# Attention rows stored in a power-of-two scale, and a running sum in the expert selection

## The chip, the cores and the metric

The kernel runs on one core of one Trainium2 chip. The metric is device time in microseconds of that core, median of several runs. One execution was also taken with the hardware profiler; its trace is what all rows below come from.

## The reference

Clustered attention is followed by a mixture of experts with a capacity. Batch 4, 8 heads, 768 tokens, head size 64, 16 clusters; 3072 tokens of 512 numbers go to 8 experts of width 1024, at most 80 tokens each.

```python
mask = q_assign[:, :, :, None] == k_assign[:, :, None, :]
scores = np.where(mask, scale * np.matmul(q, k.transpose(0, 1, 3, 2)), -1e9)
attn = np.exp(scores - np.max(scores, axis=-1, keepdims=True))
attn = attn / (np.sum(attn, axis=-1, keepdims=True) + 1e-09)
x = np.matmul(attn, v)                      # then (B*S, H*D)
...
logits = x @ w_gate                         # expert_idx = argmax, gate_w = its softmax
for e in range(E):
    tok_idx = np.where(expert_idx == e)[0]
    if len(tok_idx) > capacity:             # keep the capacity largest gate_w
        gw = gate_w[tok_idx]
        tok_idx = tok_idx[np.argpartition(-gw, capacity)[:capacity]]
    h = np.maximum(x[tok_idx] @ w1[e], 0.0)
    out[tok_idx] = gate_w[tok_idx, None] * (h @ w2[e])
```

## The kernel before

Products that need more than fp16 gives are made from two halves: a high part rounded to fp16, and the rest. `scale` (L253) makes for each batch a power of two `s` for v, from the sum of its squares, so that the halves stay within fp16; `split_v` multiplies v with it.

**Attention.** For each of 32 heads and 6 blocks of 128 keys, TensorE makes scores, ACT two exponentials (`exps`, L575: fp32 and fp16), and their difference `ll` is made on POOL or, for the tiles that `inplace` (L569) names, on DVE (`rests`, L589). TensorE sums with both halves (`av`, L596). `normalise` (L614) divides by the sum of weights (times `s`, which undoes v's scale) and stores the rows of x to a buffer `xs` in HBM. `gates` (L643) makes the gate value `G` and the one-hot `OH` of each token's expert.

**Selection.** To keep the 80 largest gates of each expert, `select` (L732) finds a threshold per expert by digits of the bits of `G`, in five levels (shift 20, 15, 10, 5, 0). `digits` (L671) makes for each level the tables `ge` and `pre` on DVE. In a level TensorE counts over 24 token blocks (L754), DVE turns counts into a digit `nf` (L781), TensorE spreads the digit into `nb` (L784), and DVE marks the tokens still `alive` (L791), which the next level's counts read. `banks` (L740) prepares the next level's `nb`: one product for the base (L744) and one for each digit so far (L746). At the end DVE converts `nb` (L798), makes masks, slot positions and, with TensorE, a table `tb` of what stands in each of the 80 slots: token number, three parts of the gate, a flag (`terms`, L705, makes the factors on POOL). `gi` (L853) are the rows to gather.

**Experts.** One unit per expert (80 rows). `gather` (L1043) is an indirect DMA from POOL. For seven of the eight experts (all but number 1, `native1`) `norms` squares the gathered rows on ACT (L1054), `factors` makes a power of two from that in four small DVE instructions (`power`, L876) and two more (L1063, L1065), `tokens` multiplies and splits into fp16 halves on DVE (L1071, L1072); `turn` transposes on TensorE (L1089), `turned` copies, `hidden` multiplies with w1 (L1118), `relu`, `rest` (`hl`, L1134), `output` with w2 (L1146), `gated` (L1171) applies gate and scales, `scatter` writes by indirect DMA (L1176). Weights come in chunks of 512 KB (`load_w`, L902): w1 needs statistics (L918, summed by L923), a scale, and a split. A chunk named in `scaled` is scaled and rounded by two ACT instructions (L1010, L1011) and its low half made by POOL (L1022); any other takes one (L1013 or L1015) and DVE makes the low half (L1024). w2 of the experts 1, 6 and 7 is split as well (L1034 or L1036, and L1040 on POOL or DVE).

**Order.** A planner, `Flow.run` (L1644), runs when the program is built. It gives each step a start by estimated durations and readiness, takes the earliest start on any engine and, among steps of that engine within `wait`, the one with the least offset `at`; so it writes the fixed order of every engine. On the chip each engine works through its order and waits where an operand isn't there. `CFG` holds the offsets (`mix`), how many rooms serve split halves and raw chunks (`slots`), and `bias`, by which the second engine of a step with two (`alt`) must be better. While the selection lane has steps, another lane's DVE step is taken only if it ends before `spare` (L1626), which is when the selection's next step can start plus `mix["spare"]`. Where TensorE would stand longer than `idle`, `fill` (L1600) puts in products that nobody reads (L1506).

Of the kernel before, what the change touches and what calls it, by code (L numbers as in the profile page):

```python
# [7 lines left out]
F32 = mybir.dt.float32  # L8
# [11 lines left out]
CFG = dict(at=dict(rest=0.54, av=3.29, norm=2.04, sm=6.87, exp=0.06, mx=-0.9), stick=0.11, wait=0.128, idle=0.4, dummy=128, bias=1.25,  # L20
           side=(9.43, 16.01, 23.62, 0.88, 28.38), prep=(-1.42, 0.49), lead=(-40, -37.0, -39.26, -37.55, -28.47),
           zero=(-14.97, 0.62, -5.05, 0.1, 4.78, 1.09, -19.25, 0.81, -3.2, 0.25, -13.65, 0.65),
           start=dict(pe=6.1, act=4.8, dve=7.5, pool=2.5, dma=0.0), warm=48, nab=6, lag=3, share=(1, 5), raws=8, slots=(19, 5), native1=(1,),
           native2=(0, 2, 3, 4, 5), early=((5, 0), 185.8), scaled=(3, 4, 5, 6, 7, 11, 13, 14, 17, 19, 20, 21, 22, 24, 27, 29),
           mix=dict(ld=-22.68, st=-20.3, hi1=-1.69, lo1=-10.0, hi2=-14.51, lo2=-5.27, xg=-21.49, xp=-17.51, out=18.38, sc=-11.74, a0=5, a1=4, a2=4, spare=-0.08))
# [11 lines left out]
class Program:  # L37
# [35 lines left out]
    def setup(self):  # L73
# [28 lines left out]
        self.OH = con.tile([P, NT, E], F16, name="OH")  # L102
        self.wgd = con.tile([P, NP, 32], F32, name="wgd")
# [149 lines left out]
    def scale(self, b):  # L253
# [30 lines left out]
        nc.vector.tensor_copy(si[:, 0:1], ti[:, 3:4])  # L284
        nc.vector.scalar_tensor_tensor(ti[:, 4:5], ti[:, 2:3], 127, si[:, 0:1], op0=ALU.add, op1=ALU.subtract)
# [283 lines left out]
    def inplace(self, g):  # L569


        n, d = CFG["share"]
        return (g + 1) * n // d > g * n // d
# [40 lines left out]
    def normalise(self, b, h):  # L614
# [3 lines left out]
        a, (_, _, s, _, ratio) = st["av"], st["s", b]  # L618
# [7 lines left out]
        nc.vector.tensor_scalar(den, a[:, :, X], 1e-9, s, op0=ALU.add, op1=ALU.mult)  # L626
# [5 lines left out]
        nc.vector.scalar_tensor_tensor(l[:, :, :, h], a[:, :, D:X], ratio, rec.unsqueeze(2).broadcast_to([P, NC, E]),  # L632
# [72 lines left out]
    def terms(self):  # L705
# [4 lines left out]
        R = w.tile([P, NT, E, 5], F16, name="R")  # L710
# [15 lines left out]
        put(0, self.tok)  # L726
        nc.gpsimd.tensor_tensor(g[:, :, 2], r1, g[:, :, 1], op=ALU.subtract)
# [4 lines left out]
    def select(self):  # L732
# [7 lines left out]
        def banks(l):  # L740

            q, nb = ps.tile([E, 36], F32, name="q", bufs=2), ps.tile([P, 3 * E + NT], F32, name="nb", bufs=2)
            if l == 0 or self.levels[l][0]:
                nc.tensor.matmul(nb[:, 0:E], lhsT=self.ones[0:E], rhs=self.view["idl"][0:E, 0:E], start=True, stop=False)  # L744
                for i, x in enumerate(nfs):
                    nc.tensor.matmul(nb[:, 0:E], lhsT=x.broadcast_to([E, P]), rhs=ids[i], start=False, stop=False)  # L746
            return q, nb

        for l, (sh, d0, ge, pre) in enumerate(self.levels):
# [6 lines left out]
            if l == 0:  # L756
                yield Step("pe", .025 * known + .2, needs=[("norm", self.B * self.H - 1)])
                q, nb = banks(0)
# [3 lines left out]
            else:  # L762
                yield Step("pe", .025 * NT, also=("dve", .55 if sh else .85), needs=[("ge", l)])
                count(0, NT)
# [8 lines left out]
                if sh == 0:  # L773
                    ti = nb_[:, E:2 * E].bitcast(I32)
                    nc.vector.tensor_scalar(ti, nb_[:, 0:E], 1024.0, None, op0=ALU.mult)
                    top = w.tile([P, E], I32, name="top")
                    nc.vector.tensor_scalar(top, ti, 5, BASE, op0=ALU.logical_shift_left, op1=ALU.bitwise_or)
# [6 lines left out]
            nc.tensor.matmul(nb[:, 0:E], lhsT=nf.broadcast_to([E, P]), rhs=ids[l], start=sh == 0, stop=True)  # L784
            q_, nb_, nj = q, nb, nk
            if sh:
                more = .18 * (l + 2) if self.levels[l + 1][0] else .02
                yield Step("dve", .43, also=("pe", more), needs=[("pre", l)])
# [35 lines left out]
        for m, s0 in enumerate(range(0, cap, P)):  # L824
# [6 lines left out]
            tb = ps.tile([P, E, 5], F32, name="tb", tag="pos")  # L831
# [22 lines left out]
            yield Step("dve", .68, key=("slots", m))  # L854
# [5 lines left out]
            nc.vector.scalar_tensor_tensor(g2, tv[:, :, 1], 1.0 / 1024.0, g1, op0=ALU.mult, op1=ALU.add)  # L860
# [89 lines left out]
    def start(self):  # L950
        self.counts = [0] * 3
        self.hp, self.y, self.xss = {}, {}, {}
        self.width = self.w1.shape[2]
        self.np = self.w1.shape[1] // P, self.w2.shape[1] // P // (self.width // self.w2.shape[2])
        for n in ("raw", "w1s", "ss", "sw", "w2s", "xg", "xt", "xp", "sx", "gs", "h", "yp"):
            setattr(self, n, {})
# [93 lines left out]
    def norms(self, u):  # L1050
        nc, w, Mb, xg = self.nc, self.mw, self.blocks[u[1]][0], self.xg[u]
        xp = self.xp[u] = self.room(4 + self.count(1) % 2, F16).rearrange("p (i d) -> p i d", i=2)
        ss = self.xss[u] = w.tile([P, 1], F32, name="xss", bufs=2)
        nc.scalar.activation(xp[0:Mb, 0], xg[0:Mb], AF.Square, accum_out=ss[0:Mb])  # L1054

    def factors(self, u):

        nc, w, (e, m) = self.nc, self.mw, u
        Mb, gi, si, gate = self.blocks[m]
        ss, bank = self.xss.pop(u), self.misc([P, 8])  # L1060
        self.power(bank[:, 4:6], bank, ss[0:Mb], Mb)
# [101 lines left out]
    def gated(self, u):  # L1163
# [6 lines left out]
        else:  # L1170
            nc.vector.tensor_scalar(y[0:Mb], yp, self.gs[u][0:Mb], self.sw[e][0:Mb, 1:2], op0=ALU.mult, op1=ALU.mult)  # L1171
# [7 lines left out]
    def experts(self):  # L1179
# [401 lines left out]
class Flow:  # L1581
# [62 lines left out]
    def run(self):  # L1644
        while True:
            ready, spare = [], self.spare()
            for n, lane in enumerate(self.lanes):
# [38 lines left out]
            if eng == "pe" and self.idle and start - self.free[eng] > CFG["idle"]:  # L1686
# [113 lines left out]
```

## Time and profile before

| | |
|---|---|
| median of 3 runs | 589.18 us (586.09 to 590.32) |
| the profiled execution | 588.15 us, its span 586.0 us |
| PE (TensorE) busy | 544.2 us, 93% |
| DVE (VectorE) busy | 449.2 us, 77% |
| ACT (ScalarE) busy | 464.8 us, 79% |
| POOL (GpSimd) busy | 423.0 us, 72% |
| mean granted TensorE clock | 0.961 |

Times of the trace count from the start of the span. PE is a matmul, PEld a weight load that can overlap it, SPq a DMA issued from SyncE. A row of a timeline gives start, duration, engine, line, operation, output and inputs with their shapes, how many were merged, and in brackets the idle time of the engine before it with what ended it. Busy time on an engine that is not the bottleneck costs nothing, and a share over the whole span mixes stages with different limits.

### The profile page before, as it was taken

What the parts mean: (1) busy time and instruction counts of PE and PEld (TensorE: products, weight loads), DVE (VectorE), ACT (ScalarE), POOL (GpSimd) and SP (SyncE); (2) the same over time, 40 slices, a digit from 0 to 9 for tenths busy, and PEclk for the clock granted to TensorE, in tenths of its full rate; (3) what the DMA queues carried; (4) which work ended last, traced back from release to release, by engine and by line L of the source; (5) the groups of instructions that cost most, each with busy time, mean ns of one, the idle gap of its engine ahead of it and who ended that gap; (6) DMA issues with size and microseconds to landing.
All of it is one profiled execution on the core that took longest, in us unless ns stands there. A gap on an engine that the chain in (4) does not pass through costs nothing. (4 is left out here: it accounts for less than half of the span.)

```text
span 586.0 us, 16832 instructions
## 1 busy us (share of the span) xinstructions
PE 544.2 (93%) x6641; PEld 438.3 (75%) x6641; DVE 449.2 (77%) x1027; ACT 464.8 (79%) x766; POOL 423.0 (72%) x273
## 2 busy tenths in 40 slices
PE   7898999999999999999999999999987838999976
PEld 6566888888888887887888888899776726866544
DVE  4876887888888887887887889787964575577992
ACT  7778788899979978997997889878684964799630
POOL 5348867699987777998776799887675742556873
PEclk9989999999999999999999999999999567999989
DMA  8679875579897547889653966385822887799501
GB/s 292 202 217 233 245 201 134 131 184 267 247 288 174 137 114 189 248 244 281 171 137 87 225 168 150 80 215 162 336 64 58 286 270 230 242 337 331 185 1 34
DMA packets 69774, 114.23 MB, mean 195 GB/s; under 512 B 7072, under 2 KB 38464, under 8 KB 69696
## 3 DMA queue, kind: packets, MB, share of 16 engines
q1 hardware_dynamic: 68672, 110.54, 66.0%
q0 software_dynamic: 1024, 2.62, 1.5%
q8 instruction: 52, 0.85, 0.6%
q14 instruction: 26, 0.21, 0.1%
HBM read 60.46 MB, written 13.89 MB: 127 GB/s over the span
## 5 line engine op out<-in xcount | busy, mean ns | idle before, releaser
L593 POOL TENSOR_TENSOR ll<-pp,hh 128x768 f16<-128x768 f32 x154 | 254.4, 1665 | 68.4 <-ACT hh L586 36.2
L530 DVE TENSOR_REDUCE mx<-sm 128x1 f32<-128x384 f32 x384 | 201.8, 551 | 48.6 <-PE sm L528 46.1
L584 ACT ACTIVATE pp<-st 128x768 f32<-128x768 f32 x154 | 124.6, 809 | 36.2 <-PE st L565 32.5
L528 PE MATMUL sm<-KAB,QAB 80*128 80x384 f32 x384 | 141.8, 395 | 2.9 <-DVE mx L530 1.4
L601 PEld LDWEIGHTS <-hh 128*128 128x128 f16 x2304 | 120.5, 98 | 25.7 <-issue 14.7
L601 PE MATMUL av<-vh,hh 128*128 128x73 f16 x1152 | 136.7, 199 | 0.0
L601 PE MATMUL av<-vl,hh 128*128 128x72 f16 x1152 | 135.5, 197 | 0.0
L601 PE MATMUL av<-vh,ll 128*128 128x73 f16 x1152 | 134.4, 198 | 1.0 <-POOL ll L593 1.0
L586 ACT ACTIVATE hh<-st 128x768 f16<-128x768 f32 x154 | 124.3, 807 | 0.0
L601 PEld LDWEIGHTS <-ll 128*128 128x128 f16 x1152 | 113.0, 98 | 1.6 <-POOL ll L593 1.5
L562 PE MATMUL st<-QAB,KAB 128*128 128x384 f32 x384 | 104.8, 354 | 2.3 <-ACT hh L586 2.0
L565 PE MATMUL st<-QAB,KAB 81*128 81x384 f32 x384 | 100.1, 342 | 0.8 <-DMA QAB<-row 0.8
L528 PEld LDWEIGHTS sm<-KAB,QAB 80*128 80x128 f32 x384 | 70.2, 189 | 24.1 <-DVE mx L530 13.8
L562 PEld LDWEIGHTS st<-QAB,KAB 128*128 128x128 f32 x384 | 67.0, 192 | 8.1 <-ACT hh L586 4.7
L565 PEld LDWEIGHTS st<-QAB,KAB 81*128 81x128 f32 x384 | 70.7, 191 | 1.2 <-DMA QAB<-row 1.1
L593 DVE TENSOR_TENSOR ll<-st,hh 128x768 f16<-128x768 f32 x38 | 36.1, 950 | 2.1 <-ACT st L586 2.0
L1022 POOL TENSOR_TENSOR w1p<-raw,w1p 128x1024 f16<-128x1024 f32 x10 | 26.1, 2606 | 14.5 <-ACT w1p L1011 12.5
L318 POOL TENSOR_TENSOR vl<-ldv,vh 128x512 f16<-128x512 f32 x24 | 27.1, 1130 | 12.6 <-ACT vh L316 12.6
L584 ACT ACTIVATE hh<-st 128x768 f16<-128x768 f32 x38 | 30.9, 812 | 5.2 <-PE st L565 5.1
L367 POOL TENSOR_TENSOR ldk<-ldk,hi 128x768 fp32r<-128x768 f32 x15 | 27.4, 1828 | 5.2 <-ACT hi L365 2.8
L586 ACT ACTIVATE st<-st 128x768 f32<-128x768 f32 x38 | 30.7, 807 | 0.0
L394 POOL TENSOR_TENSOR ldq<-ldq,hi 128x768 fp32r<-128x768 f32 x15 | 27.4, 1827 | 2.6 <-DVE vss L270 1.8
(295 smaller groups left out, 891.6 us busy)
## 6 DMA issues: line engine op xcount, KB each, us to landing
raw<-in_w_dram SPq DMA_DIRECT2D x40, 512.0 KB
KAB<-hi SPq DMA_DIRECT2D x60, 192.0 KB
QAB<-hi SPq DMA_DIRECT2D x30, 384.0 KB
room<-in_w_dram SPq DMA_DIRECT2D x20, 512.0 KB
ldk<-in_kT_dram SPq DMA_DIRECT2D x16, 384.0 KB
ldq<-in_qT_dram SPq DMA_DIRECT2D x16, 384.0 KB
ldvt<-in_vT_dram SPq DMA_DIRECT2D x12, 512.0 KB
ldv<-in_v_dram SPq DMA_DIRECT2D x12, 512.0 KB
```

Of the source, the lines that this page charges most:

```text
L318: nc.gpsimd.tensor_tensor(lo, t[:, c], hi, op=ALU.subtract)
L367: nc.gpsimd.tensor_tensor(lo, t, hi.bitcast(F32), op=ALU.subtract)
L394: nc.gpsimd.tensor_tensor(lo, t, hi.bitcast(F32), op=ALU.subtract)
L528: nc.tensor.matmul(s, lhsT=qj, rhs=k[0:D + C, 0, f * HS:(f + 1) * HS], start=True, stop=True)
L530: nc.vector.tensor_reduce(mx[:, j, f:f + 1], s, axis=AX.X, op=ALU.max)
L562: nc.tensor.matmul(s[:, f, 0:HS], lhsT=k[:, 1, ks], rhs=q[:, 1, qs], start=True, stop=False)
L565: nc.tensor.matmul(s[:, f, 0:HS], lhsT=k[0:D + C + 1, 0, ks], rhs=q[0:D + C + 1, 0, qs], start=False, stop=True)
L584: nc.scalar.activation(order[0], s, AF.Exp, scale=float(D) ** -0.5)
L586: nc.scalar.activation(order[1], s, AF.Exp, scale=float(D) ** -0.5)
L593: eng.tensor_tensor(ll, pp, hh, op=ALU.subtract)
L601: mm = lambda out, l, r, **kw: nc.tensor.matmul(out, lhsT=l, rhs=r, skip_group_check=True, **{"start": False, "stop": False, **kw})
L1022: nc.gpsimd.tensor_tensor(t[:, 1], raw, t[:, 0], op=ALU.subtract)
```

## The change

The rows of x are no longer freed of v's power of two: `normalise` leaves `s` in, and the exponent of each token block is kept in a new tile `pow`, goes through the slot table as a sixth column, and becomes part of the gate `g2`. So the gathered rows need no squares and no factors of their own: `tokens` is a copy to fp16 (DVE or ACT), `tokens2` a subtraction (DVE or POOL). In the selection one tile `nb` takes the sum of the digits of the first four levels as it grows, one product per level; the last level has its own. The last attention tile is made in place. In the planner, DVE steps of other lanes get a margin `sure` while the selection runs, the filling threshold is 0.2 in the mixture, unit 0's rows are put first, and offsets are new.

```diff
-           ... dummy=128, bias=1.25,
+           ... dummy=128, bias=1.79,
-           ... slots=(19, 5), native1=(1,),
-           ... early=((5, 0), 185.8), scaled=(3, 4, 5, 6, 7, 11, 13, 14, 17, 19, 20, 21, 22, 24, 27, 29),
-           mix=dict(ld=-22.68, st=-20.3, hi1=-1.69, lo1=-10.0, hi2=-14.51, lo2=-5.27, xg=-21.49, xp=-17.51, out=18.38, sc=-11.74, a0=5, a1=4, a2=4, spare=-0.08))
+           ... slots=(18, 6), native1=(1,),
+           ... early=((5, 0), 185.06), scaled=(0, 3, 4, 5, 6, 7, 13, 14, 17, 19, 20, 21, 22, 24, 27),
+           mix=dict(ld=-29.05, st=-20.3, hi1=-8.87, lo1=-10.0, hi2=-14.51, lo2=-5.27, xg=-22.53, xp=-22.18, out=18.35, sc=-15.51, a0=5, a1=4, a2=4, spare=-0.45, sure=0.56, gap=0.2))
...
-        nc.vector.tensor_copy(si[:, 0:1], ti[:, 3:4])
-        nc.vector.scalar_tensor_tensor(ti[:, 4:5], ti[:, 2:3], 127, si[:, 0:1], op0=ALU.add, op1=ALU.subtract)
+        nc.vector.tensor_scalar(ti[:, 4:5], ti[:, 3:4], -1, 254, op0=ALU.mult, op1=ALU.add)
+        nc.vector.tensor_copy(self.pow[:, b * NC:(b + 1) * NC], ti[:, 2:3].broadcast_to([P, NC]))
...
-        return (g + 1) * n // d > g * n // d
+        return (g + 1) * n // d > g * n // d or g == self.B * self.H * self.NC - 1
...
-        nc.vector.tensor_scalar(den, a[:, :, X], 1e-9, s, op0=ALU.add, op1=ALU.mult)
+        nc.vector.tensor_scalar(den, a[:, :, X], 1e-9, None, op0=ALU.add)
...
-        R = w.tile([P, NT, E, 5], F16, name="R")
+        R = w.tile([P, NT, E, 6], F16, name="R")
...
+        put(5, self.pow)
...
-        def banks(l):
...
+        nbs = [ps.tile([P, 3 * E + NT], F32, name=n) for n in ("nb", "nl")]
+        total = lambda nb, l, r, start: nc.tensor.matmul(nb[:, 0:E], lhsT=l, rhs=r, start=start, stop=True, skip_group_check=True)
...
-                q, nb = banks(0)
+                total(nbs[0], self.ones[0:E], self.view["idl"][0:E, 0:E], True)
...
-            nc.tensor.matmul(nb[:, 0:E], lhsT=nf.broadcast_to([E, P]), rhs=ids[l], start=sh == 0, stop=True)
+            nb = nbs[sh == 0]
+            total(nb, nf.broadcast_to([E, P]), ids[l], sh == 0)
...
-                q, nb = banks(l + 1)
...
-            tb = ps.tile([P, E, 5], F32, name="tb", tag="pos")
+            tb = ps.tile([P, E, 6], F32, name="tb", tag="pos")
...
-            nc.vector.scalar_tensor_tensor(g2, tv[:, :, 1], 1.0 / 1024.0, g1, op0=ALU.mult, op1=ALU.add)
+            nc.vector.scalar_tensor_tensor(g1, tv[:, :, 1], 1.0 / 1024.0, g1, op0=ALU.mult, op1=ALU.add)
+            ti = tv[:, :, 0:2].bitcast(I32)
+            nc.vector.tensor_scalar(ti[:, :, 0], tv[:, :, 5], -1.0, 254.0, op0=ALU.mult, op1=ALU.add)
+            nc.vector.tensor_scalar(ti[:, :, 1], ti[:, :, 0], 23, None, op0=ALU.logical_shift_left)
+            nc.vector.tensor_tensor(g2, g1, tv[:, :, 1], op=ALU.mult)
...
-    def norms(self, u):
...
-    def factors(self, u):
...
+    def tokens(self, u, eng):
+        nc, Mb, xg = self.nc, self.blocks[u[1]][0], self.xg.pop(u)
+        xp = self.xp[u] = self.room(4 + self.count(1) % 2, F16).rearrange("p (i d) -> p i d", i=2)
+        if eng == "act":
+            nc.scalar.copy(xp[0:Mb, 0], xg[0:Mb])
+        else:
+            nc.vector.tensor_copy(xp[0:Mb, 0], xg[0:Mb])
+        self.xgs = xg
+    def tokens2(self, u, eng):
+        Mb, xg, xp = self.blocks[u[1]][0], self.xgs, self.xp[u]
+        eng.tensor_tensor(xp[0:Mb, 1], xg[0:Mb], xp[0:Mb, 0], op=ALU.subtract)
...
-            nc.vector.tensor_scalar(y[0:Mb], yp, self.gs[u][0:Mb], self.sw[e][0:Mb, 1:2], op0=ALU.mult, op1=ALU.mult)
+            nc.vector.tensor_scalar(y[0:Mb], yp, gate[0:Mb, e:e + 1], self.sw[e][0:Mb, 1:2], op0=ALU.mult, op1=ALU.mult)
...
-            p = U / NB * i + A["xp"]
+            p = U / NB * i + A["xp"] if i else -900.0
...
-                yield Step("act", .72, needs=[("xg", i), *back(i, 2, "tp")], at=p, seq=True)
-                self.norms(u)
-                yield Step("dve", 1.0, needs=[("slots", u[1])], at=p, seq=True, take="misc", give="misc")
-                self.factors(u)
-                yield Step("dve", 1.25, key=("xr", i), at=p, seq=True, two=True)
-                self.tokens(u)
+                yield Step("dve", .48, alt=("act", .5), needs=[("xg", i), *back(i, 2, "tp")], at=p, seq=True, two=True)
+                self.tokens(u, flow.which)
+                yield Step("dve", .75, alt=("pool", 1.3), key=("xr", i), at=p, seq=True, two=True)
+                self.tokens2(u, nc.vector if flow.which == "dve" else nc.gpsimd)
...
+                    if eng == "dve" and lane is not self.first and self.first and self.first.look():
+                        start = max(start, t + CFG["mix"]["sure"])
...
-            if eng == "pe" and self.idle and start - self.free[eng] > CFG["idle"]:
+            if eng == "pe" and self.idle and start - self.free[eng] > (CFG["mix"]["gap"] if self.first else CFG["idle"]):
```

## Rows read from the trace of the kernel before

**Rows 1.** Windows: busy us (count) of PE, PEld, DVE, ACT, POOL; clock; DMA share; GB/s.
```profile
540.00:550.00 10.00, 10.00 (x120) 5.97 (x119) 8.87 (x9) 9.44 (x15) 9.53 (x4) 1.00 0.89 330
...
560.00:570.00 10.00, 6.84 (x22) 3.63 (x21) 10.00 (x9) 2.50 (x4) 6.26 (x3) 0.83 0.01 2
```

**Rows 2.** Timeline, the last experts: start us, duration us, engine, line, operation.
```profile
564.82 0.71 PE L1146 MATMUL yp<-w2p,hl 128*80 128x512 f32 x1 [3.16 <-DVE hl L1134]
...
567.60 1.27 DVE L1024 SCALAR_TENSOR_TENSOR w1p<-raw,sw,w1p 128x1024 f16<-128x1024 f32 x1
...
571.61 3.61 PE L1118 MATMUL hp<-xt,w1p 128*128 128x80 f16 x96
```

**Rows 3.** Timeline, the last tiles of the attention.
```profile
441.27 0.96 DVE L593 TENSOR_TENSOR ll<-st,hh 128x768 f16<-128x768 f32 x1 [1.19 <-ACT st L586]
...
445.31 1.64 POOL L593 TENSOR_TENSOR ll<-pp,hh 128x768 f16<-128x768 f32 x1 [0.88 <-POOL ll L593]
```

**Rows 4.** Timeline, the selection's levels.
```profile
453.61 0.42 DVE L791 SCALAR_TENSOR_TENSOR alive<-dug,nb 128x96 f16<-128x96 f32 x2 [0.44 <-PE nb L784]
...
454.35 0.80 PE L754 MATMUL q<-dug,alive 128*8 128x31 f16 x24
...
454.92 0.35 DVE L698 TENSOR_TENSOR dug<-dp,K 128x186 f16<-128x186 int32 x1
...
459.54 0.42 DVE L791 SCALAR_TENSOR_TENSOR alive<-dug,nb 128x96 f16<-128x96 f32 x2 [0.46 <-PE nb L784]
...
459.79 1.42 PE L746 MATMUL nb<-K,nf 8*128 8x8 f32 x6
...
461.14 0.80 PE L754 MATMUL q<-dug,alive 128*8 128x31 f16 x24
...
463.15 0.42 DVE L791 SCALAR_TENSOR_TENSOR alive<-dug,nb 128x96 f16<-128x96 f32 x2 [0.92 <-PE nb L784]
...
463.58 0.80 PE L754 MATMUL q<-dug,alive 128*8 128x31 f16 x24
```

**Rows 5.** Timeline, the end of the digits.
```profile
464.96 0.59 PE L784 MATMUL nb<-K,nf 8*128 8x8 f32 x2
...
467.58 0.16 DVE L923 TENSOR_REDUCE wss<-wss 128x1 f32<-128x4 f32 x1 [2.91 <-ACT room L918]
467.65 0.17 DVE L798 CAST nb<-nb 128x8 int32<-128x8 f32 x1
```

**Rows 6.** Timeline, unit 0 from its gather to its hidden matmuls.
```profile
474.67 1.09 POOL L1047 DMA_INDIRECT room<-xs,gi  x1 [4.06 <-DVE g L858]
...
480.70 0.62 ACT L1054 ACTIVATE room<-room 80x512 f16<-80x512 f32 x1
...
481.45 0.16 DVE L879 TENSOR_SCALAR tot<-xss 80x1 int32<-80x1 int32 x1 [3.02 <-ACT room L1054]
...
482.30 0.14 DVE L1065 TENSOR_TENSOR gs<-g,tot 80x1 f32<-80x1 f32 x1
482.37 1.71 DVE L1024 SCALAR_TENSOR_TENSOR w1p<-raw,sw,w1p 128x1024 f16<-128x1024 f32 x1
...
484.00 0.47 DVE L1071 TENSOR_SCALAR room<-room,sx 80x512 f16<-80x512 f32 x1
484.50 0.75 DVE L1072 SCALAR_TENSOR_TENSOR room<-room,sx,room 80x512 f16<-80x512 f32 x1
...
487.26 4.62 PE L1118 MATMUL hp<-xt,w1p 128*128 128x80 f16 x96
```

**Rows 7.** The gathers' line L1047, eight issues: from issue to landing.
```profile
DMA to landing us min/median/max: 5.2/6.6/7.6
```

**Rows 8.** Timeline, a split beside a POOL operation.
```profile
502.22 2.13 POOL L1022 TENSOR_TENSOR w1p<-raw,w1p 128x1024 f16<-128x1024 f32 x1 [3.38 <-ACT w1p L1011]
502.22 2.41 DVE L1071 TENSOR_SCALAR room<-room,sx 80x512 f16<-80x512 f32 x1
```

**Rows 9.** Groups by line and shape from 451 us on: busy us, mean ns.
```profile
L1071 DVE TENSOR_SCALAR room<-room,sx 80x512 f16<-80x512 f32 x7 | 7.6, 1084 | 0.0
```

More of the change, by code (lines that the diff above doesn't have):

```diff
@@ L19 @@
 BASE = 0x3C000000
-CFG = dict(at=dict(rest=0.54, av=3.29, norm=2.04, sm=6.87, exp=0.06, mx=-0.9), stick=0.11, wait=0.128, idle=0.4, dummy=128, bias=1.25,
+CFG = dict(at=dict(rest=0.54, av=3.29, norm=2.04, sm=6.87, exp=0.06, mx=-0.9), stick=0.11, wait=0.128, idle=0.4, dummy=128, bias=1.79,
            side=(9.43, 16.01, 23.62, 0.88, 28.38), prep=(-1.42, 0.49), lead=(-40, -37.0, -39.26, -37.55, -28.47),
            zero=(-14.97, 0.62, -5.05, 0.1, 4.78, 1.09, -19.25, 0.81, -3.2, 0.25, -13.65, 0.65),
-           start=dict(pe=6.1, act=4.8, dve=7.5, pool=2.5, dma=0.0), warm=48, nab=6, lag=3, share=(1, 5), raws=8, slots=(19, 5), native1=(1,),
-           native2=(0, 2, 3, 4, 5), early=((5, 0), 185.8), scaled=(3, 4, 5, 6, 7, 11, 13, 14, 17, 19, 20, 21, 22, 24, 27, 29),
-           mix=dict(ld=-22.68, st=-20.3, hi1=-1.69, lo1=-10.0, hi2=-14.51, lo2=-5.27, xg=-21.49, xp=-17.51, out=18.38, sc=-11.74, a0=5, a1=4, a2=4, spare=-0.08))
+           start=dict(pe=6.1, act=4.8, dve=7.5, pool=2.5, dma=0.0), warm=48, nab=6, lag=3, share=(1, 5), raws=8, slots=(18, 6), native1=(1,),
+           native2=(0, 2, 3, 4, 5), early=((5, 0), 185.06), scaled=(0, 3, 4, 5, 6, 7, 13, 14, 17, 19, 20, 21, 22, 24, 27),
+           mix=dict(ld=-29.05, st=-20.3, hi1=-8.87, lo1=-10.0, hi2=-14.51, lo2=-5.27, xg=-22.53, xp=-22.18, out=18.35, sc=-15.51, a0=5, a1=4, a2=4, spare=-0.45, sure=0.56, gap=0.2))
 PE, EV = "PE", "EV"
@@ L102, in setup @@
         self.OH = con.tile([P, NT, E], F16, name="OH")
+        self.pow = con.tile([P, NT], F16, name="pow")
         self.wgd = con.tile([P, NP, 32], F32, name="wgd")
@@ L617, in normalise @@
         X = D + E
-        a, (_, _, s, _, ratio) = st["av"], st["s", b]
+        a, back = st["av"], st["s", b][4]
         if h % 2 == 0:
@@ L763, in select @@
                 yield Step("pe", .025 * NT, also=("dve", .55 if sh else .85), needs=[("ge", l)])
+                q = ps.tile([E, 36], F32, name="q", bufs=2)
                 count(0, NT)
@@ L783, in select @@
             yield Step("pe", .18)
-            nc.tensor.matmul(nb[:, 0:E], lhsT=nf.broadcast_to([E, P]), rhs=ids[l], start=sh == 0, stop=True)
-            q_, nb_, nj = q, nb, nk
+            nb = nbs[sh == 0]
+            total(nb, nf.broadcast_to([E, P]), ids[l], sh == 0)
+            q_, nj = q, nk
             if sh:
-                more = .18 * (l + 2) if self.levels[l + 1][0] else .02
-                yield Step("dve", .43, also=("pe", more), needs=[("pre", l)])
+                yield Step("dve", .43, needs=[("pre", l)])
                 alive = [w.tile([P, half, E], F16, name="alive", bufs=4) for _ in range(2)]
@@ L853, in select @@
             nc.vector.tensor_scalar(gi, tv[:, :, 0], float(self.N // 2), None, op0=ALU.add)
-            yield Step("dve", .68, key=("slots", m))
+            yield Step("dve", .95, key=("slots", m))
             nc.vector.tensor_scalar(t1, tv[:, :, 2], 1.0 / 1024.0, None, op0=ALU.mult)
@@ L951, in start @@
         self.counts = [0] * 3
-        self.hp, self.y, self.xss = {}, {}, {}
+        self.hp, self.y = {}, {}
         self.width = self.w1.shape[2]
         self.np = self.w1.shape[1] // P, self.w2.shape[1] // P // (self.width // self.w2.shape[2])
-        for n in ("raw", "w1s", "ss", "sw", "w2s", "xg", "xt", "xp", "sx", "gs", "h", "yp"):
+        for n in ("raw", "w1s", "ss", "sw", "w2s", "xg", "xt", "xp", "h", "yp"):
             setattr(self, n, {})
```

29 lines of the change are left out of this document (4 added, 25 removed).

## The prediction

> **What bounds the kernel now.** I read the page first: which engine is full in which slice. Then the windows of the last 140 us, the timeline there engine by engine, and the waits. The change leaves the attention stage (up to 447 us) as it is, but for its last tile, so everything is decided between 445 and 586 us. Three stretches have different limits.
>
> From 447 to 474 us one chain runs alone: gates, five levels of digit selection, slot positions. It hops between VectorE and TensorE; nothing else can start the experts. From 474 to 487 us it goes on as gather, norms, factors, split, transpose, first hidden matmul; TensorE stands nearly still. From 487 us on TensorE is busy without a hole until 561 us, and again from 565 us. But the preparation of the weights is close behind: in 540 to 550 us the DMA share is 0.89, ACT is at 9.44 and POOL at 9.53 of 10 us; from 560 to 570 us DVE is full (10.00) [rows 1]. The reader is to see in the timeline how late the weights come: expert 7's last low half is ready at 568.87 (567.60 + 1.27) and its hidden matmuls start at 571.61, so the slack is 2.7 us [rows 2]. At 564.82 TensorE had waited 3.16 us for DVE's `hl` [rows 2]. So an earlier start of the experts counts in full only if the preparation moves forward too.
>
> **The change, part by part.** All terms are made against the profiled execution, 588.15 us (span 586.0 and 2.15 around it). It lies 1.0 us under the median of the runs shown, 589.18.
>
> *Last tile in place.* The last `ll` runs on POOL from 445.31 for 1.64 us, and the last sums wait for it. DVE made such a tile in 0.96 [rows 3]. Gain 0.7 us, on the chain.
>
> *Running sum.* Before, TensorE rebuilds the sum for the next level with 1 + l further products behind the one that DVE waits for, and the counts stand behind them in TensorE's order. Level 1's counts start at 454.35, though DVE's `alive` was done at 454.03 (453.61 + 0.42): 0.3 us. Two rounds on, `alive` is done at 459.96 and the counts start at 461.14, held by the L746 products (1.42 us): 1.2 us. Before the last round, which has nothing to rebuild, `alive` ends at 463.57 and the counts start at 463.58: 0.0 [rows 4]. Three rounds are held, the products growing by one each, so the middle one is taken midway: 0.3 + 0.7 + 1.2 = 2.2 us gained.
>
> Against it stands the planner. `spare` goes from -0.08 to -0.45 and `sure` keeps any other DVE step back by 0.56 beside a selection step. The digit steps are such other steps. Today L698 (0.35 us, at 454.92) fits in while TensorE counts [rows 4]; a later place is behind `alive`, where the next counts wait for it. One such slip costs the 0.35 and a handover, about 0.5 us; four can happen. Bounds 0 and 2 us lost; I take one, 0.5, since the digits are only due a round later.
>
> *The stray sum at the end of the selection.* The last product of the digits starts at 464.96, but DVE converts it at 467.65, because L923 (weight statistics) stood in front and waited 2.91 us for ACT [rows 5]. The product is a 0.6 us affair, so about 2 us are lost. `sure` is the part of the change that acts on this order, but 0.56 us of margin is less than the 2 us by which ACT was late. Bounds 0 and 2.0; I take the middle, 1.0.
>
> *Gathered rows.* Before, for unit 0: gather issued at 474.67; landing takes at least 5.2 us [rows 7], so 479.9; ACT squares at 480.70; six DVE instructions of [80x1] from 481.45 to 482.44; a weight instruction (L1024) queued in front of the split until 484.08; then L1071 0.47 and L1072 0.75, done at 485.25; the hidden matmuls at 487.26 [rows 6]. After, squares and factors are gone and the place of unit 0 is first (-900): landing 479.9, a copy like L1071, a subtraction like L1072, done at 481.15. Gain 4.1 us. Both ends: if the copy waits as the squares did, to 480.70, 3.3; if it also waits for a POOL operation as L1071 did later (2.41 instead of 0.48, beside L1022) [rows 8], 1.4. I take 4.1, for the copy stands first in its queue. If DVE stands at its head waiting for the landing, what queues behind are two low halves of expert 0 (1.27 each), due only when the rows are transposed: at most 2.5 us of the 4.1 would go.
>
> The landing time carries this term, and here a rule differs from the row. The rows say 5.2 to 7.6 us over eight gathers [rows 7]. The Trainium skill, DMA: Bandwidth & Descriptors, Anatomy of one DMA, fits about 2.0 us plus the bytes at 436 GB/s; for 80 rows of 2 KB that is 2.4 us, an estimate from that page. By it the sum would be 2.8 us larger. The measured row decides.
>
> For the other six split units the same six instructions (about 1.0 us of DVE) and the square (0.62 us of ACT) go, hidden behind TensorE except where supply is tight. In the full stretch lie units 4 to 7: 4 x 1.0 us of DVE.
>
> *Costs that I set at nothing.* Three more [80x8] DVE operations behind the slots (the six factors took 0.16 each): the flight of the gather covers them; uncovered, 0.5 us. `pow` in scale(): as many small instructions as before, four times. A sixth product in terms(): POOL does it when the selection begins, and the slot products at the selection's end are the first to need it; `tb` with 48 instead of 40 columns is short against its weight loads. `gated` has the same instruction. One raw slot more lets one load go earlier, one split slot fewer delays one later: nothing either way. Chunk 0 goes to POOL; 11 and 29 come to DVE. For expert 7 this is 1.27 us more on a full DVE [rows 2], so I count it against the 4.0: 2.7 us left. The larger `bias` sends fewer splits to DVE in the other direction, unpriced. Retuned offsets and more filler products (`gap`) change orders I cannot read from this trace: 2 us either way.
>
> **Sum.** First hidden matmul: 0.7 + 2.2 - 0.5 + 1.0 + 4.1 = 7.5 us earlier. Supply: it starts from the same selection, so 0.7 + 2.2 - 0.5 + 1.0 = 3.4, and 2.7 less work in the full stretch: 6.1. The end moves by something between 6.1 and 7.5, since 2.7 us of slack can be drawn on but turn into waits. I take 6.5: 588.15 - 6.5 = 581.7.
>
> **Rivals.** (a) *Supply holds the end.* If the weights come when they come (DMA share and ACT near full in 540 to 550), the end moves only by the slack of 2.7 and a little: 588.15 - 2.7 = 585.5. For it: the slack itself. Against: loads wait for rooms that earlier work frees, so they move with the selection.
>
> (b) *The selection doesn't get shorter.* Digits move behind `alive` four times (2.0 us) and L923 stays in front: a gain of 0.7 + 0.2 is left there, plus 4.1 in the rows, and supply allows 0.9 + 2.7 = 3.6: 584.6.
>
> (c) *Slower: copy against POOL.* L1071 beside a POOL operation took 1.9 us longer (2.41 against 0.48) [rows 8]. The copy is of the same kind. If all four copies in the full stretch meet one, where one did before (the mean of L1071 over seven units is 1.08 us) [rows 9], DVE gets 3 x 1.9 = 5.7 us more against the 2.7 saved, and the two tail subtractions of w2 that POOL holds slip with it: the end moves by 5.7 - 2.7 = 3.0 the wrong way, 591.2. It decides from the third such meeting on, provided the head start is used up by then. The page for this is the Trainium skill, GPSIMD Engine Reference, Specifications: GpSimd shares its SBUF interfaces with VectorE, in conflict with two-port modes and with two SBUF inputs; by that rule both copy and subtraction on DVE are exposed, and the trace agrees (2.41). Against the rival: L1071 is as exposed today.
>
> (d) *More than the sum.* The 3.16 us wait at 564.82 [rows 2] goes with the new order: 581.7 - 3.2 = 578.5.
>
> **Chances.** The forecast 0.45, (a) 0.23, (b) 0.10, (c) 0.10, (d) 0.12. One per cent, about what a measurement of this kernel can tell from no change, is 5.9 us, so 582.3 is the line. Three quarters of the forecast's own range, 579.5 to 584.5, lie under it when weighted to its middle: 0.34; with (d) 0.46. Slower by over 1%, past 594.0, is the half of (c) in which the retuned order costs its 2 us too and the splits of w2 another one: 0.05. The rest, 0.49, is within 1%. The range reaches from beyond (d) to between (a) and (c): 577.0 to 588.5; it leaves out (c) and the far end of (d).
>
> **What would show it.** Right: the counts start within 0.1 us of `alive` in all rounds; the last `ll` on DVE; `gi` some 3.4 us earlier; TensorE's first hidden matmul near 479.8 instead of 487.26; no [80x1] operations between the hidden stages; expert 7's last low half near 562. Wrong: digits between `alive` and the counts; a DVE instruction waiting for ACT in front of the last conversion; copies of 2 us and more; or an early first hidden matmul followed by new holes in TensorE from 520 us on, which would be (a). The forecast falls as a whole if the new offsets delay loads, which no row of before can show.

## The result, and the profile after

The changed kernel takes 580.73 us (median of 4 runs, 580.18 to 582.73) against 588.88 us beside it: ratio 0.9886, 95% interval 0.9849 to 0.9923. The forecast was 581.7. The profiled execution takes 580.86 us, its span is 579.1 (before 586.0): 6.9 us less. The number was nearly met, but by other terms than those of the sum.

Three marks of each trace show where the 6.9 us lie. The mark `OH` (L667 before, L669 after) is the last row ahead of the selection: 451.04 before, 449.96 after. The first hidden matmul starts at 487.26 [rows 6] and 486.29. From `OH` to there it takes 36.2 us before and 36.3 after: **the front half past `OH`, for which I had forecast 6.8 us (7.5 less the last tile's 0.7), gained nothing.** From the first hidden matmul to the end of the span it takes 98.7 and 92.8: 5.9 us come from there. The other 1.1 us is `OH` itself.

The selection after, from the timeline, as answer to [rows 3 to 5] (start us, duration us, engine, line, operation; in brackets the idle time ahead and what ended it):

```profile
444.93 0.96 DVE L595 TENSOR_TENSOR ll<-st,hh 128x768 f16<-128x768 f32 x1 [2.98 <-ACT st L588]
...
454.65 1.35 PE L1498 MATMUL tot<-K,one 128*128 128x128 f16 x11
454.76 0.24 DVE L781 TENSOR_SCALAR_CACHE_REDUCE j<-q,rem 8x31 f32<-8x31 f32 x1 [0.36 <-PE q L752]
...
455.94 0.49 PE L745 MATMUL nb<-K,nf 8*128 8x8 f32 x2
456.36 1.40 PE L1498 MATMUL tot<-K,one 128*128 128x128 f16 x22
456.47 0.42 DVE L791 SCALAR_TENSOR_TENSOR alive<-dug,nb 128x96 f16<-128x96 f32 x2 [1.47 <-PE nb L745]
...
457.00 0.35 DVE L700 TENSOR_TENSOR dug<-dp,K 128x186 f16<-128x186 int32 x1
457.69 0.76 PE L752 MATMUL q<-dug,alive 128*8 128x31 f16 x24
...
465.50 0.38 PE L745 MATMUL nl<-K,nf 8*128 8x8 f32 x2
...
465.92 0.17 DVE L797 CAST nl<-nl 128x8 int32<-128x8 f32 x1 [0.95 <-PE nl L745]
```

The digit of this level is there at 455.0 (454.76 + 0.24), but the product that spreads it starts at 455.94, behind eleven filler products (L1498) of TensorE. Then `alive` ends at 456.89, and the next counts start at 457.69, not 0.1 us later. In between DVE makes the next level's digits (L698, L700, done at 457.35), and TensorE runs 22 more fillers, until 457.76. It is the fillers that hold the counts, as e6 below shows. Both waits together cost more than the removed products gave. The last line is the better half: DVE converts `nl` 0.4 us after its product starts, where it was 2.7 us [rows 5].

Unit 0 after, answering to [rows 6 and 7]: the timeline, then the gathers' line in 472 to 478 us, then a window (busy us of PE, PEld, DVE, ACT, POOL; granted clock; DMA share; GB/s):

```profile
470.81 0.33 SPq L906 DMA_DIRECT2D raw<-in_w_dram  x1
471.24 0.89 SPq L906 DMA_DIRECT2D dug<-in_w_dram  x2
...
473.03 1.09 POOL L1051 DMA_INDIRECT room<-xs,gi  x1 [2.25 <-DVE g L857]
...
480.88 0.42 DVE L1061 CAST room<-room 80x512 f16<-80x512 f32 x1 [4.68 <-DMA room<-xs,gi]
...
481.33 0.69 DVE L1066 TENSOR_TENSOR room<-room,room 80x512 f16<-80x512 f32 x1
...
482.92 3.04 PE L1498 MATMUL tot<-K,one 128*128 128x128 f16 x27 [0.30 <-DVE sw L886]
485.75 0.74 PE L1076 MATMUL tp<-K,room 80*128 80x80 f32 x4
486.29 3.90 PE L1112 MATMUL hp<-xt,w1p 128*128 128x80 f16 x96
...
DMA to landing us min/median/max: 7.8/8.0/8.1
...
482.00:484.00 2.00, 1.70 (x20) 1.58 (x20) 1.81 (x7) 1.28 (x2) 0.91 (x1) 0.50 0.15 40
```

The gather is issued 1.64 us earlier, yet its rows are there only at 480.9: three weight chunks (1.5 MB) had been issued in the 2.2 us ahead of it. No square and no [80x1] operation stands behind it any more, and the split is done at 482.02 (before 485.25). Then TensorE runs 27 fillers in 3.04 us, at a granted clock of 0.50, the level of 1.2 GHz, and transposes unit 1 before it starts on unit 0's hidden matmuls, 4.3 us after the split instead of 2.0.

The tail of before, in rows that were not shown (timeline; DVE, then POOL, then TensorE), is where most of the 5.9 us lie:

```profile
554.44 4.10 DVE L1040 TENSOR_TENSOR w2p<-room,w2p 128x1024 fp32r<-128x1024 f32 x1
558.46 3.15 DVE L1024 SCALAR_TENSOR_TENSOR w1p<-raw,sw,w1p 128x1024 f16<-128x1024 f32 x1
561.53 2.83 DVE L1015 TENSOR_SCALAR w1p<-raw,sw 128x1024 f16<-128x1024 f32 x1
564.29 0.48 DVE L1134 SCALAR_TENSOR_TENSOR hl<-hp,hh 128x320 fp32r<-128x320 f32 x1
...
555.07 2.37 POOL L1040 TENSOR_TENSOR w2p<-room,w2p 128x1024 fp32r<-128x1024 f32 x1
557.96 2.56 POOL L1022 TENSOR_TENSOR w1p<-raw,w1p 128x1024 f16<-128x1024 f32 x1 [0.52 <-ACT w1p L1011]
560.49 3.32 POOL L1040 TENSOR_TENSOR w2p<-raw,w2p 128x1024 fp32r<-128x1024 f32 x1
...
560.86 0.80 PE L1146 MATMUL yp<-w2p,hh 128*80 128x512 f32 x1
...
568.38 0.39 PE L1146 MATMUL yp<-w2p,hl 128*80 128x512 f32 x1
```

Three DVE instructions, each beside a POOL subtraction, took 10.1 us; the shortest that these forms take elsewhere is 1.2, 1.3 and 0.7. They stood in front of `hl`, for which TensorE waited 3.16 us [rows 2]. The products behind that wait then ran slowly, at a granted clock of 0.66 over 564 to 569 us. The first eleven products of this output take from 560.86 to 568.77, 7.9 us with the wait. After:

```profile
556.09 3.37 DVE L1028 SCALAR_TENSOR_TENSOR w1p<-dug,sw,w1p 128x1024 f16<-128x1024 f32 x1
...
558.59 0.56 PE L1112 MATMUL hp<-xt,w1p 128*128 128x80 f16 x11
559.51 3.22 PE L1112 MATMUL hp<-xt,w1p 128*128 128x80 f16 x85 [0.37 <-DVE w1p L1028]
562.56 0.44 PE L1140 MATMUL yp<-w2p,hh 128*80 128x512 f32 x1
...
564.93 0.39 PE L1140 MATMUL yp<-w2p,hl 128*80 128x512 f32 x1
```

Expert 7's last low half is ready at 559.46 (before 568.87), its hidden matmuls now stand in front of that output, and the same eleven products take 2.8 us (562.56 to 565.32). That is 5.1 us of the 5.9; the first hidden stage, 3.90 instead of 4.62 us at a higher clock (0.88 instead of 0.57 in 486 to 490 us), is another 0.7.

### The profile page after: what moved, and what is told of

Read it like the earlier page. It is cut to its first block, busy times and chain, and to the rows that moved or that the text cites. A ratio compares the mean times of both kernels' runs of the same rounds, so it can differ in the third digit from the quotient of the medians.

```text
span 579.1 us, 17054 instructions
## 1 busy us (share of the span) xinstructions
PE 550.0 (95%) x6781; PEld 446.0 (77%) x6781; DVE 436.5 (75%) x987; ACT 462.4 (80%) x753; POOL 417.0 (72%) x273
## 5 line engine op out<-in xcount | busy, mean ns | idle before, releaser
L1498 PEld LDWEIGHTS <-one 128*128 128x128 f16 x455 | 32.0, 109 | 4.5 <-issue 2.2
L1026 POOL TENSOR_TENSOR w1p<-raw,w1p 128x1024 f16<-128x1024 f32 x9 | 21.5, 2387 | 14.7 <-ACT w1p L1015 8.9
```

Source lines behind the costliest of these rows:

```text
L1026: nc.gpsimd.tensor_tensor(t[:, 1], raw, t[:, 0], op=ALU.subtract)
L1498: nc.tensor.matmul(out, lhsT=by, rhs=self.K16[:, 0:n], start=alone, stop=alone, skip_group_check=True)
```

## The experiments

Every kernel was run beside the kernel before, in three sets (e1 to e4, e5 to e8, e9 to e12); across sets the ratios compare better than the medians. The marks are those of each one's profiled execution, one per kernel, while the executions of one kernel differ by up to 9 us (e3: 579.81 to 588.50). The attention stage ahead of `OH` is nearly the same work in all, yet ends between 448.2 and 454.1 us, so the last two columns say more than a span does.

| kernel | median us | ratio to before, 95% | `OH` at | `OH` to first hidden | first hidden to end |
|---|---|---|---|---|---|
| before | 588.88 | 1 | 451.04 | 36.2 | 98.7 |
| after | 580.73 | 0.9886 [0.9849, 0.9923] | 449.96 | 36.3 | 92.8 |
| e1 old work, new plan | 590.48 | 1.0027 [0.9989, 1.0064] | 451.64 | 35.9 | 101.2 |
| e2 new work, old plan | 585.52 | 0.9960 [0.9926, 0.9993] | 450.55 | 33.5 | 97.9 |
| e3 rows alone | 580.90 | 0.9892 [0.9807, 0.9976] | 450.12 | 34.3 | 93.6 |
| e4 running sum alone | 602.75 | 1.0238 [1.0173, 1.0303] | 449.68 | 36.3 | 111.4 |
| e5 digits first | 586.64 | 0.9990 [0.9952, 1.0029] | 449.89 | 34.2 | 99.5 |
| e6 no fill in selection | 586.04 | 0.9994 [0.9962, 1.0026] | 448.20 | 36.4 | 99.4 |
| e7 turn after hidden | 581.72 | 0.9915 [0.9883, 0.9947] | 454.13 | 35.4 | 93.7 |
| e8 digits and turn | 583.52 | 0.9927 [0.9887, 0.9967] | 453.74 | 34.1 | 95.5 |
| e9 before, POOL writes zeros | 580.01 | 0.9866 [0.9785, 0.9948] | 449.37 | 33.4 | 93.7 |
| e10 after, POOL writes zeros | 576.25 | 0.9764 [0.9688, 0.9841] | 451.72 | 30.2 | 92.6 |
| e11 e5, POOL writes zeros | 574.36 | 0.9755 [0.9677, 0.9834] | 451.15 | 29.3 | 92.6 |
| e12 rows and last tile, old plan | 588.88 | 0.9966 [0.9917, 1.0015] | 450.92 | 34.0 | 102.5 |

### Work and plan apart: e1 to e4

e1 is the kernel before with the new `CFG`, `sure`, `gap` and unit 0's place; e2 the changed kernel with the old ones. e3 has the stored scale, the copies and the exponent in the table, and nothing else; e4 the running sum and nothing else.

```diff
 # e4, against the kernel before
-        def banks(l):
+        nbs = [ps.tile([P, 3 * E + NT], F32, name=n) for n in ("nb", "nl")]
+        total = lambda nb, l, r, start: nc.tensor.matmul(nb[:, 0:E], lhsT=l, rhs=r, start=start, stop=True, skip_group_check=True)
...
+            nb = nbs[sh == 0]
+            total(nb, nf.broadcast_to([E, P]), ids[l], sh == 0)
```

> The kernel before with all its work (squares, factors, rebuilt sums, last tile on POOL), but with the new offsets and the new planner rules (margin, filling threshold, unit 0 first). Theory A, the forecast's: the gain is a head start of the first unit that comes from less work, so without it nothing is gained, 588 to 591 us, and the digits behind alive may cost 1 to 2 us. Theory B, read from the trace of after: only 2.7 us of the gain are a head start and 4 us come from the tail, where expert 7's weights are ready early enough for its hidden matmuls to stand before expert 6's output. If the offsets alone do that (B1), 583 to 586 us; if it needs the lighter DVE (B2), 587 to 590 us and TensorE still waits 3 us for hl near the end.

> The changed kernel's work (stored scale, running sum, last tile in place) with the offsets and planner rules of before. Theory A: rows 4.1, sum 2.2, tile 0.7 and no digits behind alive: first hidden matmul 7 us earlier, 581 to 583 us. Theory B1 (the tail's gain is the offsets'): 584 to 587 us, with the wait for hl near the end still there. Theory B2 (it is the lighter DVE's): 580 to 583 us with the wait gone. In all of them the rounds of the selection are about 2.2 us shorter than before in total, since the old margin lets the digits in front of alive.

> The kernel before with the stored scale alone (no squares, no factors, sixth slot column), old sums, old planner. Theory A: unit 0's rows 4.1 us earlier, 584 to 585.5 us. Theory B: the gather's landing and unit 1's transposes, which stand in front of unit 0's hidden matmuls on TensorE, hold the start, so the first hidden matmul moves by 1 us or less; end 585 to 588 us under B1, 582 to 585 us under B2 (six fewer DVE instructions per unit free the tail).

> The kernel before with the running sum alone. Theory A: counts follow alive at once, gi 2.2 us earlier, end 586 to 587 us. Theory B: the same 2.2 us in the selection, as nothing of the new margin is there to push the digits behind alive; the end moves by no more than the tail lets it, 585.5 to 589 us. If the rounds are not shorter here either, the rebuilt sums were never the limit and the step of the forecast was wrong at its root.

The plan alone gains nothing, the rows alone as much as the whole change within their intervals, all the new work with the old plan only 0.4%, and the running sum alone costs 2.4%. In the selection the sum does most of what was forecast: its rounds are 2.65 us apart (`alive` at 452.45, 455.11, 457.76, 460.42), those of before up to 3.6. The three rounds take 8.0 us instead of 9.5, a gain of 1.6 where 2.2 was forecast; e2 shows the same 1.6. So the new margin and threshold, not the sum, made the rounds of the changed kernel long. At `gi` nothing is left of it in either: counted from `OH` it comes at 23.4 (e4) and 23.3 us (e2), before at 23.2, because the conversion stands behind a sum of statistics again, 3.9 and 4.4 us after its product starts. e3 gains 3.7 us from gather to split, near the 4.1 forecast for the rows, and loses 1.3 of them again from split to hidden, behind 36 fillers of 2.18 us.

Where e4 loses is in its tail (timeline; DVE, POOL, TensorE):

```profile
537.75 5.43 DVE L1019 SCALAR_TENSOR_TENSOR w1p<-raw,sw,w1p 128x1024 f16<-128x1024 f32 x1
...
553.63 5.59 DVE L1067 SCALAR_TENSOR_TENSOR room<-room,sx,room 80x512 f16<-80x512 f32 x1
...
560.28 0.14 DVE L918 TENSOR_REDUCE wss<-wss 128x1 f32<-128x4 f32 x1
...
537.89 4.20 POOL L1017 TENSOR_TENSOR w1p<-raw,w1p 128x1024 f16<-128x1024 f32 x2
...
554.01 4.66 POOL L1035 TENSOR_TENSOR w2p<-room,w2p 128x1024 fp32r<-128x1024 f32 x2
...
560.48 0.59 PE L923 MATMUL tot<-wss,ones 128*128 128x1 f32 x2 [8.89 <-DVE wss L918]
```

A split that takes 0.75 elsewhere took 5.59 and ended behind two POOL subtractions. Behind it on DVE stood the sum of an expert's weight statistics, for it TensorE waited 8.9 us, and the output products queued behind. At most 4.8 of the 8.9 are this split's delay; no run took POOL's subtractions out of e4, so that they cost it its tail is read from these rows, not tested. e1 looks alike (its L1015 took 5.68 us at 552.13, and TensorE then waited 3.4 us for low halves of w1).

### The front half: e5 to e8

e5 takes the digits' steps out of `sure` and gives them the old limit; e6 puts in no fillers while the selection runs; e7 lets TensorE transpose unit 1 only after unit 0's first hidden step; e8 is e5 with e7. All against the changed kernel.

```diff
 # e5
-                    if eng == "dve" and lane is not self.first and self.first and self.first.look():
+                    if eng == "dve" and lane is not self.first and lane is not self.digs and self.first and self.first.look():
 # e6
-            ... start - self.free[eng] > (CFG["mix"]["gap"] if self.first else CFG["idle"]):
+            ... start - self.free[eng] > (99.0 if self.first and self.first.look() else CFG["mix"]["gap"] if self.first else CFG["idle"]):
 # e7
+                ... *([("hid", 0, 0)] if i == 1 else [])
```

> The changed kernel, with the digit steps alone exempt from the new margin, so that they can stand before alive again; all other rules are as in the changed kernel. If digits behind alive cost the running sum its gain, the counts follow alive within 0.3 us where they now come 0.7 to 0.9 us later, gi is 1.5 to 3 us earlier and the end 0 to 2.5 us earlier (578 to 580.5 us). If the fillers before the counts or the spread are the cause, gi moves by less than 0.7 us.

> The changed kernel without filler products while the selection lane has steps. If the fillers delay the spread of the digit (0.93 us after the digit in level 1 against 0.29 before) and the counts, gi comes about 0.5 to 1 us earlier in spite of slower products at a low clock; if the clock that they keep up is worth more (0.96 of full in 455 to 470 us, 0.50 before; spread 0.38 against 0.59 us), gi comes 1 to 2 us later. End within 1 us of the changed kernel either way, since the first hidden matmuls wait for the gathers.

> The changed kernel, with unit 1's transposes held back on TensorE until the first half of unit 0's hidden matmuls. In the changed kernel unit 0's transposed rows are ready at 483.4 us, but its hidden matmuls start at 486.29, behind unit 1's transposes, which wait for their gather. Theory: they start 2.5 us earlier. If the head start carries through, 578 us; if supply holds the end (slack of a few us at most behind the last weights), 579.5 to 581 us, with new holes in TensorE later.

> Both edits, digits exempt from the margin and unit 1's transposes behind unit 0's hidden matmuls. If the start limits the end, 576 to 578 us; if supply does, 579 to 581 us, like the changed kernel.

With the digits in front of `alive` again (e5), the rounds are 2.65 us apart and the front half is 2.1 us shorter, at a clock of 0.50 in 455 to 470 us where the changed kernel had 0.96. By itself this would blame the digits. But with them moved, the planner also puts only 6 fillers in front of the counts, where the changed kernel has 11 to 23. e6 tells the two apart, for it leaves the digits behind `alive` and takes only the fillers out (DVE, then TensorE):

```profile
453.25 0.42 DVE L791 SCALAR_TENSOR_TENSOR alive<-dug,nb 128x96 f16<-128x96 f32 x2 [0.68 <-PE nb L745]
...
453.78 0.35 DVE L700 TENSOR_TENSOR dug<-dp,K 128x186 f16<-128x186 int32 x1
...
453.56 0.94 PE L752 MATMUL q<-dug,alive 128*8 128x31 f16 x24 [0.35 <-DVE alive L791]
```

The counts start 0.1 us before the second half of `alive` ends (453.67) and 0.6 us before the digits are done (454.13): only the last 6 of the 24 token blocks read tables that are made that late. The rounds are 2.5 to 2.6 us apart, shorter than e5's, and from `OH` to the last digit's product it takes 12.1 us (12.6 in e5, 13.9 before, 15.5 in the changed kernel). So the digits' late place costs at most 0.14 us a round (the counts take 0.94 us instead of 0.80); what held the rounds were the fillers that the planner put into the time it kept for the digits.

e6's front half is no shorter all the same (36.4): a sum of statistics stands in front of the last conversion again, as in [rows 5], and waits 5.68 us for ACT; the conversion starts at 466.01, 5.7 us after its product. e7 was a miss: the transposes it moves were not what held the first hidden matmul. It takes 3.7 us from split to hidden there (4.3 in the changed kernel); the 27 fillers still stand in front, 3.04 us long. e8 missed both of its ranges: its front half is 34.1 us like e5's, its tail 95.5.

And none of the head starts reached the end. e5, 2.2 us ahead of the changed kernel at the first hidden matmul, is behind it by 5.9 us in the median (ratios 0.9990 and 0.9886). Its timeline (DVE, POOL, TensorE):

```profile
540.72 5.28 DVE L1040 CAST w2p<-raw 128x1024 fp32r<-128x1024 f32 x1
...
547.07 3.35 DVE L1044 TENSOR_TENSOR w2p<-room,w2p 128x1024 fp32r<-128x1024 f32 x1
550.34 0.14 DVE L927 TENSOR_REDUCE wss<-wss 128x1 f32<-128x4 f32 x1
...
541.01 2.14 POOL L1026 TENSOR_TENSOR w1p<-raw,w1p 128x1024 f16<-128x1024 f32 x1
543.10 2.34 POOL L1044 TENSOR_TENSOR w2p<-raw,w2p 128x1024 fp32r<-128x1024 f32 x1
...
550.54 0.59 PE L932 MATMUL tot<-wss,ones 128*128 128x1 f32 x2 [4.58 <-DVE wss L927]
```

The same chain as in e4: DVE held by POOL, statistics late, TensorE held in its order.

### The collision itself: e9 to e12

In e9, e10 and e11 (before, after, e5) POOL writes zeros where it made low halves; it reads nothing then, and the planned order of every engine stays. e12 is e3 with the last tile in place.

```diff
-            nc.gpsimd.tensor_tensor(t[:, 1], raw, t[:, 0], op=ALU.subtract)
+            nc.gpsimd.memset(t[:, 1], 0.0)
...
+        if eng is self.nc.gpsimd:
+            eng.memset(lo.bitcast(F32), 0.0)
+        else:
             eng.tensor_tensor(lo, raw, hi.bitcast(F32), op=ALU.subtract)
```

> The kernel before, with one thing left out: where GpSimd made a low half of a weight (high minus stored, two operands read from SBUF), it now writes zeros and reads nothing; the order of every engine is as it was. The low halves on GpSimd are thus missing from the result. Theory A, the collision of GpSimd and VectorE sets the supply of the experts' weights: from 470 to 586 us the VectorE instructions of the kernel before ran 18.5 us longer than the shortest of their forms did, in 11 instructions that stand beside a GpSimd subtraction. That goes, and the 3.2 to 4.0 us in which TensorE waited for hl at the tail go with it: 588.9 - 3.6 = 585.3 us. Theory B, ACT, the transfers and TensorE's order set the end: within 1 us of 588.9.

> The changed kernel with the same part left out (zeros in the low halves that GpSimd makes). Theory A: VectorE gets back 12.4 us, but TensorE has only 0.6 us of waits left behind the first hidden matmul, so the time hardly moves: 579.5 to 580.7. Theory B: the same. The run is the yardstick for the next: the two differ by nothing but the start of the experts.

> The digits-first kernel (first hidden matmul 2.2 us before the changed kernel's, yet 5.9 us behind it at the end) with the same part left out. Theory A: its wait of 4.58 us for the weight sum at 545.9, behind a VectorE copy of 5.28 us and a subtraction of 3.35 us beside GpSimd, goes away, and the 2.2 us head start comes through: about 578, 2 us under the changed kernel with the same part left out. Theory B: the head start is lost as before, 585 to 587.

> Stored scale and last tile in place, with the old sums and the old offsets: the two parts that paid. If the 0.7 to 1.1 us of the last tile come through, 580.9 - 0.9 = 580.0 us, span 577.1. If the order of the tail decides and not the start, within 1 us of 580.9 either way, or some us slower should a new meeting of GpSimd and VectorE open a hole.

In the tail theory A held: 98.7 becomes 93.7, 99.5 becomes 92.6, and 92.8 stays 92.6. The hole at `hl`, e5's wait of 4.58 us and the loss against the changed kernel are gone. Adding up each DVE row's time over the shortest of its form, where that is over 0.3 us, the stretch from 535 us on falls from 11.9 us to 0.6 (e9), from 8.7 to 2.2 (e10) and from 12.9 in e5 to 1.2 (e11). In the profiled executions a head start now counts in full: e11's first hidden matmul starts 1.40 us before e10's (480.47, 481.87), 0.6 of it at `OH`, and its span is 1.4 us shorter; the runs of the two overlap, so their medians do not settle it. With POOL's subtractions out, the change itself is worth 3.8 us (580.01 in e9, 576.25 in e10, every run of e10 below every run of e9).

All three are faster than I expected, by 3 to 5 us, mainly because the front half got shorter too. From e10 (its timeline, then the window that answers to the one of after):

```profile
462.03 2.22 SPq L906 DMA_DIRECT2D room<-in_w_dram  x3
464.87 0.33 SPq L906 DMA_DIRECT2D raw<-in_w_dram  x1
465.30 0.89 SPq L906 DMA_DIRECT2D dug<-in_w_dram  x2
...
474.08 1.09 POOL L1054 DMA_INDIRECT room<-xs,gi  x1 [11.95 <-DVE g L857]
...
477.44 0.42 DVE L1064 CAST room<-room 80x512 f16<-80x512 f32 x1 [0.19 <-DMA room<-xs,gi]
...
480.03 1.67 PE L1501 MATMUL tot<-K,one 128*128 128x128 f16 x27 [0.54 <-issue]
...
481.87 3.61 PE L1115 MATMUL hp<-xt,w1p 128*128 128x80 f16 x96
...
482.00:484.00 2.00, 2.00 (x61) 2.00 (x59) 2.00 (x3) 1.90 (x3) 1.70 (x2) 1.00 0.70 271
```

POOL is done with w2's low halves by 462 instead of 471 us, their rooms come free, the six loads go out from 462 to 466 us instead of 464 to 472, and the gather finds the way free: its rows are there after 3.4 us instead of 7.8. TensorE has stood less, its clock is 1.00, and the 27 fillers take 1.67 us instead of 3.04. That is 4.5 us at the landing and 1.0 from split to hidden, of the 6.2 by which the front half is shorter. Other runs agree on the landing: where the three chunks were issued 3.1 to 4.3 us ahead of the gather (before, e1 to e4, e12) it took 4.6 to 5.2 us, where they were issued 1.3 to 2.2 us ahead (the changed kernel) 7.8, and with over 10 us between (e9) 3.3.

e12 was a miss: with the last tile in place the planner writes another tail, and that falls into the collision (TensorE waits 3.0 us for the `w1p` of the last hidden matmuls):

```profile
563.40 2.98 DVE L1033 SCALAR_TENSOR_TENSOR w1p<-raw,sw,w1p 128x1024 f16<-128x1024 f32 x1
...
562.49 6.11 POOL L1049 TENSOR_TENSOR w2p<-raw,w2p 128x1024 fp32r<-128x1024 f32 x2
...
566.45 4.61 PE L1117 MATMUL hp<-xt,w1p 128*128 128x80 f16 x85 [3.03 <-DVE w1p L1033]
```

**What is not settled.** Writing zeros also makes POOL's step shorter (0.97 us instead of 2.1 to 4.6) and lets it go before the high half is there. The rows show DVE held, but how much of the 5 to 7 us in the tail is DVE's wait and how much POOL's own time was not told apart. Nor is the number of collisions the whole story: by the reckoning above the stretch from 535 us on has 11.9 us before, 8.7 after, 9.9 in e3, 5.3 in e6, yet e3's tail is short and e6's is not (TensorE waits 3.4 us for statistics there). It counts where the collision falls. And since any change of work lets the planner write a new tail, e3 shows that the rows' change leads to a good one, not that its saved instructions are what pays.

## Why the prediction was right, and where it was not

*Last tile in place: 0.7.* `OH` is 1.08 us earlier and the last `ll` is on DVE, as forecast. But `OH` lies anywhere in 5.9 us over the fourteen traces, and e12 shows no gain: the term can't be seen.

*Running sum: 2.2 less 0.5.* The mechanism of the 2.2 was right and its size was 1.6 (e2, e4). The term against it failed. From `OH` to the last digit's product it takes 15.5 us, before 13.9 (464.96 less 451.04): 1.6 lost where 1.7 was to be gained. I had named the digits behind `alive`, "where the next counts wait for it", and priced one slip of four at 0.5. All four came, but the counts do not wait for them (e6). The cost came from the fillers in front of the counts and of the digit's product, which I had put under "orders I cannot read": without them the same stretch takes 12.1 us, 3.4 less.

*Stray sum: 1.0.* 2.3, from 2.7 to 0.4: above the upper bound of 2.0. It came back with 5.7 in e6, which has the same margin, so what kept it away here is not shown.

*Selection, in sum 3.4 at `gi`.* 474.22 became 472.58: 1.6, of which 1.1 is `OH`.

*Gathered rows: 4.1, giving 7.5 at the first hidden matmul.* 1.6 were gained from gather to split, 2.3 lost again from split to hidden. The step that failed is "landing takes at least 5.2 us": that was unit 0's own landing before, with three weight chunks issued 3.1 to 4.0 us ahead of it, and I kept it for a gather that was to be issued earlier, closer behind the same loads. It took 7.8. The Trainium skill, DMA: Bandwidth & Descriptors, Anatomy of one DMA, gives 2.4 us for this size, an estimate from that page; e9's 3.3 and e10's 3.4, with the loads out of the way, are the nearest that runs here came to it.

*Supply: 6.1.* Its argument, selection plus 2.7 us of DVE work, fell with the selection. What made the tail shorter was the order: hidden 7 stands in front of output 6. DVE is busy 29.96 us in 535 to 575, before 35.67; by the reckoning above, 3.2 of these 5.7 us are shorter waits for POOL, and the 2.5 left are near the 2.7 of less work that I had counted.

*Rivals.* (d) came true, and by more than its 3.16 us (5.1), because the slow products behind the wait went with it. (b) came near in size, 1.6 instead of 0.9 at `gi`, but not by its mechanism: the statistics did not stay in front, and the digits were not what cost. (a) is half right: supply does hold the end (e5, e6), but in e5, where e11 tests it, the cause is neither the transfers nor ACT. (c) had the right mechanism and the wrong place. I asked only whether the new copies would meet POOL. Two of seven do (1.51 and 2.37 us instead of 0.41), and one subtraction (2.13 instead of 0.68), but the splits of w1 and w2 meet it too, in both kernels, and there it costs the path. On this the Trainium skill, SBUF — State Buffer, SBUF: two separate sides, says that GpSimd and VectorE (in a two-port mode or with two SBUF inputs) hold the shared port pair for a whole instruction and that the other blocks fully. The trace agrees that DVE blocks fully, even through two POOL instructions (5.28, 5.43 and 5.59 us). It does not show that the first to start wins: in e5 the DVE row starts at 540.72, the POOL row at 541.01, though starts on POOL are rough in the profile.

So the time was met by luck, by two errors that cancelled: 7.5 us forecast up to the first hidden matmul, where 1.0 came, all of it ahead of `OH`; and a gain of 5.9 us behind it, which the sum did not have and rival (d) had in part.

## What to carry to other kernels

Where DVE and POOL both prepare operands, look first for DVE rows far above the shortest of their form beside POOL rows: a late tail, and a head start that does not reach the end, can both come from there. Measure from a mark inside the trace (here the end of the gates and the first hidden matmul), since the stage ahead wanders by more than the change is worth. An early issue is an early landing only if the bulk loads issued just ahead of it move as well. Before blaming an operand for a late product, look at what stands in front of it in its own engine's order, fillers too, and take that out alone.

## What was not expected of the hardware

- One DVE instruction waits through a run of POOL instructions: 5.28, 5.43, 5.59 and 5.68 us for work of 0.7 to 1.3 us.
- One indirect gather of 80 rows took 3.4 us to land (e10) or 7.8 (after), with the DMA share in 474 to 478 us at 0.39 or 0.92.
- A granted clock of 0.96 instead of 0.50 over the selection made its small products shorter (0.38 us instead of 0.59), but e5 and e6 at the lower clock had the shorter rounds: on a chain that hops between engines the order counted for more than the clock.
